# One concatenated FFN weight tensor, loads cut where a buffer is full, and two blocks of w_down loaded early in sixteen small DMAs

## The chip, the cores and the metric

The kernel runs on one core of a Trainium2 chip. The metric is device time in microseconds. The kernel before was timed in three runs: 815.88, 816.25 and 816.37 us, median 816.25 us. One further execution was taken with the hardware profiler; it is the source of all rows below.

## The reference

One token `x` of 1024 numbers goes through two branches. Branch a is attention with cached keys and values: 32 query heads, 4 key/value heads, 65,536 positions, head size 128, everything in float32.

```
q = (x @ wq) in 32 heads;  k, v = caches, each of 4 heads shared by 8 query heads
a = softmax(q k^T / sqrt(128)) v @ wo
```

Branch b is a feed-forward network (FFN) of width 3584 with a router weight and a residual:

```
r = x @ w_r
b = x + sigmoid(r) * ((silu(x @ w_gate) * (x @ w_up)) @ w_down)
g = sigmoid(sum(x * gate_w))
out = g * a + (1 - g) * b
```

With a single token the router's choice of the top token is always that token. The weights and the caches together are 346 MB, and each byte is used once.

## The kernel before

All large loads go through one pool, `stream`, with two buffers of 16,384 float32 a partition (64 KB a partition, 8 MB a buffer). `room` takes the next buffer, `load` takes one and fills it with one DMA. All of these DMAs are issued by SP (SyncE) in the order of the program. A DMA into a buffer waits until TensorE has read the buffer's previous contents; so two large loads are under way or in use at any time. The order of the program is the order of each engine's queue; no planner moves anything.

The four key/value heads are a loop over `g`. For each: `queries` (32 matmuls, L131), then four loads of keys with two chunks of 8192 positions each (`score_chunk`, L150), the maximum over all chunks (`neg_max`), four loads of values with two chunks each (`value_chunk`, L179), and `project`, which multiplies with this head's part of `wo` into the accumulator `att` (L202). The parts of wo for head g and of wq for head g + 1 come together in a full buffer, `wo_wq`. For the last head there is no next wq, and `wo3` alone is loaded: 4 MB into a buffer of 8 MB (`load(wo3, HG, D)`).

Behind the loop follows the FFN. `up_proj` runs twice, for w_gate and w_up. Each time it makes two loads of four rows of the weight (row: 3584 numbers a partition, 7 MB a load of four) and 64 matmuls a load (L239, sixteen a row). The result goes from PSUM to `row` through ScalarE (L244), and is turned by 14 small matmuls (L247). Then w_down comes in 28 blocks of 1024 numbers a partition (512 KB a block), in two buffers of 14 blocks: the first in one DMA, the second in six of 6, 4, 2, 1, 1/2 and 1/2 blocks (L270, list `cuts`). The two halves of the last block split it by output quarters. Each block takes four matmuls into `y` (L281), one for each quarter of the output, of 256 columns each.

`x_row`, four rows of 256 numbers, is loaded right behind the first w_down load (L272). VectorE makes `res` of it (L275, L276), adds `y` (`fin`, L286), and SP stores the output (L287).

The lines that matter below are SP's issues L71, L270 and L272, in this order; the matmuls L202, L239 and L281 that wait for the loads; and the instruction queue of TensorE, whose 3134 matmuls and 3134 weight loads are fetched from memory by the same DMA engines while the kernel runs.

Of the kernel before, what the change touches and what calls it, by code (L numbers as in the profile page):

```python
# [9 lines left out]
F32 = mybir.dt.float32  # L10
# [4 lines left out]
P = 128  # L15
D = 1024
G = 4
HG = 8
DH = 128
SK = 65536  # L20
F = 3584
# [6 lines left out]
KB = D // P  # L28
NQ = D // 4
FB = F // P  # L30
# [2 lines left out]


@with_exitstack
def gated_mix_kernel(ctx: ExitStack, tc: tile.TileContext, x, vecs, k_t, v, wq0, wo_wq, wo3, w_gate, w_up, w_down, out):

# [13 lines left out]
    nc = tc.nc  # L54
    const = ctx.enter_context(tc.tile_pool(name="const", bufs=1))
# [7 lines left out]
    def room(*shape):  # L63
        t = stream.tile([P, W], F32, name="st", tag="st")
        names = " ".join("abcd"[: len(shape)])
        t = t[:, : math.prod(shape)]
        return t.rearrange(f"p ({names}) -> p {names}", **dict(zip("abcd", shape))) if len(shape) > 1 else t

    def load(src, *shape):
        t = room(*shape)  # L70
        nc.sync.dma_start(t, src)  # L71
        return t
# [4 lines left out]
    x_row = const.tile([P, NQ], F32, name="x_row")  # L77
# [19 lines left out]
    xp = const.tile([P, KB, 32], F32, name="xp")  # L97
# [7 lines left out]
    hp = const.tile([P, FB, 32], F32, name="hp")  # L105
# [8 lines left out]
    ps = ps_1.tile([P, P], F32, name="ps_m", tag="m")  # L114
# [12 lines left out]
    def queries(g, wq_t):  # L127
        ps = ps_s.tile([P, 512], F32, name="ps_q", tag="s")
        for k in range(KB):
            for j in range(4):  # L130
                nc.tensor.matmul(  # L131
                    ps[32 * j : 32 * j + 32, :NQ], xp[:, k, :], wq_t[:, k, j * NQ : (j + 1) * NQ],
                    start=(k == 0), stop=(k == KB - 1),
                )
        q_sb = work.tile([P, NQ], F32, name="q_sb")
        nc.vector.tensor_copy(q_sb, ps[:, :NQ])  # L136
        pt = ps_1.tile([P, P], F32, name="ps_m", tag="m")
        for e in range(2):
            nc.tensor.matmul(pt[:, 4 * e : 4 * e + 4], q_sb[:, e * DH : (e + 1) * DH], sel4, start=True, stop=True)
        for s in range(4):  # L140
            nc.vector.tensor_copy(
                qp[:, g % 2, s, 8 * s : 8 * s + 8].rearrange("p (j e) -> p e j", e=2),
                pt[:, :HG].rearrange("p (e j) -> p e j", e=2),
            )

    def score_chunk(g, c, kt, mx):
        ps = ps_s.tile([P, 512], F32, name="ps_s", tag="s")
        for s in range(4):
            for j in range(4):
                nc.tensor.matmul(  # L150
                    ps[32 * j : 32 * j + 32, :], qp[:, g % 2, s, :], kt[:, s, j, :], start=(s == 0), stop=(s == 3)
                )
        t = scores.tile([P, 512], F32, name="s", tag="s")
        nc.scalar.activation(t, ps, AF.Copy)  # L154
        nc.vector.tensor_reduce(mx[:, c : c + 1], t, AX.X, ALU.max)  # L155
        return t

    def neg_max(mx):

        m1 = work.tile([P, 1], F32, name="m1")  # L160
        nc.vector.tensor_reduce(m1, mx, AX.X, ALU.max)
        md = work.tile([P, P], F32, name="md")
        nc.vector.tensor_scalar_mul(md, ident, m1)
        ps = ps_1.tile([P, P], F32, name="ps_m", tag="m")
        nc.tensor.matmul(ps, ones, md, start=True, stop=True)
        mh = work.tile([P, HG], F32, name="mh")
        nc.vector.tensor_reduce(mh, ps.rearrange("p (a h) -> p h a", h=HG), AX.X, ALU.max)
        nc.vector.tensor_mul(mh, mh, nsel)
        nb = work.tile([P, 1], F32, name="nb")
        nc.vector.tensor_reduce(nb, mh, AX.X, ALU.add)  # L170
        return nb

    def value_chunk(g, c, t, vt, nb, sums, acc):
        nc.scalar.activation(t, t, AF.Exp, bias=nb, scale=SCALE, accum_out=sums[:, c : c + 1])  # L174
        pt = work.tile([P, 512], F32, name="pt", bufs=3)
        nc.vector.transpose(pt, t)  # L176
        for m in range(NM):
            j = m % 4
            nc.tensor.matmul(  # L179
                acc[32 * j : 32 * j + 32, :], pt[:, 32 * m : 32 * m + 32], vt[:, 4 * m : 4 * m + 4, :],  # L180
                start=(c == 0 and m < 4), stop=(c == NCH - 1 and m >= NM - 4),
            )

    def project(g, acc, sums, wo_t):
# [15 lines left out]
        for h in range(HG):  # L200
            for j in range(4):
# [2 lines left out]
                    start=(g == 0 and h == 0), stop=(g == G - 1 and h == HG - 1),  # L204
                )

    for g in range(G):
        queries(g, wq_t)
        mx = work.tile([P, NCH], F32, name="mx")
        s_t = []  # L210
        for c in range(NCH):
            if c % 2 == 0:
                kt = load(k_t[g, c // 2], 2, 4, 4, 512)
            s_t.append(score_chunk(g, c, kt[:, c % 2], mx))
        nb = neg_max(mx)
        sums = work.tile([P, NCH], F32, name="sums")
        acc = ps_o.tile([P, 512], F32, name="acc", tag="o")
        for c in range(NCH):
            if c % 2 == 0:
                vt = load(v[g, c // 2], 2, NB, DH)  # L220
            value_chunk(g, c, s_t[c], vt[:, c % 2], nb, sums, acc)
        if g < G - 1:
            both = load(wo_wq[g], 2, 8, 1024)
            wo_t, wq_t = both[:, 0], both[:, 1]
        else:
            wo_t = load(wo3, HG, D)
        project(g, acc, sums, wo_t)

    def up_proj(w):

        ps = ps_1.tile([P, 2, 512], F32, name="ps_f", tag="f")
        n = F // 8
        for k0 in range(0, KB, 4):
            wt = load(w[:, k0 : k0 + 4, :], 4, F)
            for k in range(4):
                for e in range(2):
                    for j in range(4):
                        at = (2 * j + e) * n
                        nc.tensor.matmul(  # L239
                            ps[32 * j : 32 * j + 32, e, :n], xp[:, k0 + k, :], wt[:, k, at : at + n],  # L240
                            start=(k0 + k == 0), stop=(k0 + k == KB - 1),
                        )
        row = work.tile([P, 2 * n], F32, name="row")
        nc.scalar.activation(row.rearrange("p (e n) -> p e n", e=2), ps[:, :, :n], AF.Copy)  # L244
        pt = ps_s.tile([P, 512], F32, name="ps_t", tag="s")
        for m in range(FQ):
            nc.tensor.matmul(pt[:, 4 * m : 4 * m + 4], row[:, m * P : (m + 1) * P], sel4, start=True, stop=True)  # L247
        return pt[:, :FB]


    gps = up_proj(w_gate)
    hid = const.tile([P, FB], F32, name="hid")
    nc.scalar.activation(hid, gps, AF.Exp, scale=-1.0)
    nc.vector.tensor_scalar_add(hid, hid, 1.0)
    nc.vector.reciprocal(hid, hid)
    nc.vector.tensor_mul(hid, gps, hid)
    ups = up_proj(w_up)
    nc.vector.tensor_mul(
        hp[:, :, 0].rearrange("p (j m) -> p m j", j=4), ups.rearrange("p (m j) -> p m j", j=4),
        hid.rearrange("p (m j) -> p m j", j=4),  # L260
    )


    y = ps_o.tile([P, NQ], F32, name="y", tag="o")
    halves = [room(FB // 2, D) for _ in range(2)]
    cuts = [(0, 14, 0, 4), (14, 20, 0, 4), (20, 24, 0, 4), (24, 26, 0, 4), (26, 27, 0, 4), (27, 28, 0, 2), (27, 28, 2, 4)]
    for b0, b1, j0, j1 in cuts:
        i = b0 // (FB // 2)
        at = slice(b0 - i * (FB // 2), b1 - i * (FB // 2))
        nc.sync.dma_start(halves[i][:, at, j0 * NQ : j1 * NQ], w_down[:, b0:b1, j0 * NQ : j1 * NQ])  # L270
        if i == 0:
            nc.sync.dma_start(x_row.rearrange("(j r) n -> j r n", r=32)[:, 0, :], x.rearrange("(j n) -> j n", j=4))  # L272

    res = const.tile([P, NQ], F32, name="res")
    nc.vector.tensor_scalar_mul(res, x_row, rest[:, 0:1])  # L275
    nc.vector.scalar_tensor_tensor(res, att, gate, res, op0=ALU.mult, op1=ALU.add)  # L276
    for b0, b1, j0, j1 in cuts:
        i = b0 // (FB // 2)
        for b in range(b0, b1):
            for j in range(j0, j1):  # L280
                nc.tensor.matmul(  # L281
                    y[32 * j : 32 * j + 32, :], hp[:, b, :], halves[i][:, b - i * (FB // 2), j * NQ : (j + 1) * NQ],
                    start=(b == 0), stop=(b == FB - 1),
                )
    fin = const.tile([P, NQ], F32, name="fin")
    nc.vector.scalar_tensor_tensor(fin, y, rest[:, 1:2], res, op0=ALU.mult, op1=ALU.add)  # L286
    nc.sync.dma_start(out.rearrange("(j n) -> j n", j=4), fin.rearrange("(j r) n -> j r n", r=32)[:, 0, :])  # L287
# [30 lines left out]
```

## Time and profile before

| | |
|---|---|
| median of three runs | 816.25 us |
| profiled execution | 815.95 us, of which its span 814.2 us |
| TensorE matmul busy | 397.8 us, 49% of the span |
| mean granted TensorE clock | 0.73 |
| bytes moved by DMA | 346.47 MB, mean 426 GB/s |
| chain that ended last | DMA 72%, PE 25%, ACT 2%, DVE 1% |
| first data | some 1.7 us after the start of the span |
| last w_down data in use | 810.27 us (last group of matmuls) |
| output stored by | 814.2 us |

The span runs from the first instruction to the last; about 1.7 us of the execution lie around it. Sixteen DMA engines move all data. A load of 128 partitions puts eight rows on each of them, one after the other; a load is usable when the slowest of the sixteen has finished. "DMA share" in a row is the mean busy share of these engines in a stretch. Because a packet is counted in the stretch in which it starts, short stretches after a restart can show more than 1.

### The profile page before, as it was taken

The numbers are of one execution on the slowest core, as the hardware profiler recorded it, in microseconds if no ns is written. First come the engines' busy times: TensorE is split into PE (matmuls) and PEld (weight loads), VectorE is DVE, ScalarE is ACT, GpSimd is POOL, SyncE is SP. The second block draws the span as 40 slices with busy tenths as digits, with TensorE's granted clock in tenths as the row PEclk, the third lists the DMA queues.
The fourth block names the chain that finished last, engine by engine and source line by source line (L and its number), as shares of the span: only waits on it lengthen the run. The fifth ranks groups of instructions, "written<-read, shape, count | busy, mean of one in ns | idle before, by whom it ended". The sixth has DMA issues, their size and how long they took to land.

```text
span 814.2 us, 6731 instructions
## 1 busy us (share of the span) xinstructions
PE 397.8 (49%) x3134; PEld 129.6 (16%) x3134; DVE 64.4 (8%) x149; ACT 45.6 (6%) x101; POOL 0.7 (0%) x6
## 2 busy tenths in 40 slices
PE   3444444444444554454454554454444444645457
PEld 1111111112111111122111111131111111211123
DVE  1000120000000200000000200000001100000000
ACT  0000020000000300000000300000001200000000
POOL 0000000000000000000000000000000000000000
PEclk9677777676677667767777777767767766857669
DMA  9999999999999999999999999999999999899997
GB/s 413 413 460 410 419 455 422 439 425 426 442 431 442 419 432 435 438 432 426 441 432 425 435 431 432 442 415 445 426 435 439 419 445 419 355 424 448 415 428 293
DMA packets 7099, 346.47 MB, mean 426 GB/s; under 512 B 920, under 2 KB 928, under 8 KB 1312
## 3 DMA queue, kind: packets, MB, share of 16 engines
q1 hardware_dynamic: 6928, 346.04, 98.6%
q8 instruction: 24, 0.39, 0.2%
q10 hardware_dynamic: 144, 0.01, 0.0%
q14 instruction: 3, 0.02, 0.0%
HBM read 346.05 MB, written 0.00 MB: 425 GB/s over the span
## 4 chain that ended last, share of the span: by engine, by line
DMA 72%; PE 25%; ACT 2%; DVE 1%; issue 0%; SPq 0%; ACTq 0%
DMA st<-in_k_t 29%; DMA st<-in_v 22%; DMA st<-in_wo_wq 11%; PE acc L179 9%; PE ps_s L150 9%; DMA st<-in_w_gate 4%; DMA st<-in_w_up 3%; DMA st<-in_w_down 3%; PE att L202 3%; PE ps_f L239 2%; ACT s L174 1%; PE ps_q L131 1%; SPq L270 0%; DVE mx L155 0%; PE y L281 0%
## 5 line engine op out<-in xcount | busy, mean ns | idle before, releaser
L150 PE MATMUL ps_s<-st,qp 128*32 128x512 f32 x1024 | 145.9, 734 | 162.1 <-DMA st<-in_k_t 162.1
L179 PE MATMUL acc<-st,pt 128*32 128x512 f32 x1024 | 148.5, 745 | 123.2 <-DMA st<-in_v 123.2
L150 PEld LDWEIGHTS ps_s<-st,qp 128*32 128x32 f32 x1024 | 40.0, 131 | 264.7 <-issue 264.7
L179 PEld LDWEIGHTS acc<-st,pt 128*32 128x32 f32 x1024 | 38.4, 134 | 230.0 <-issue 185.1
L239 PE MATMUL ps_f<-st,xp 128*32 128x448 f32 x256 | 34.7, 712 | 36.8 <-DMA st<-in_w_gate 22.6
L154 ACT ACTIVATE s<-ps_s 128x512 f32<-128x512 f32 x32 | 19.1, 597 | 567.9 <-PE ps_s L150 567.9
L155 DVE TENSOR_REDUCE mx<-s 128x1 f32<-128x512 f32 x32 | 22.0, 686 | 290.0 <-ACT s L154 290.0
L176 DVE STREAM_TRANSPOSE pt<-s 128x512 f32<-128x512 f32 x32 | 22.7, 711 | 177.2 <-PE acc L179 173.4
L202 PE MATMUL att<-st,op 128*32 128x256 f32 x256 | 21.3, 505 | 25.1 <-DMA st<-in_wo_wq 24.6
L174 ACT ACTIVATE s<-s,nb 128x512 f32<-128x512 f32 x32 | 22.6, 707 | 10.4 <-DVE nb L170 10.4
L281 PE MATMUL y<-st,hp 128*32 128x256 f32 x224 | 16.0, 431 | 7.5 <-DMA st<-in_w_down 7.5
L239 PEld LDWEIGHTS ps_f<-st,xp 128*32 128x32 f32 x256 | 9.8, 140 | 60.7 <-issue 27.5
L131 PE MATMUL ps_q<-st,xp 128*32 128x256 f32 x256 | 17.1, 427 | 0.0
L202 PEld LDWEIGHTS att<-st,op 128*32 128x32 f32 x256 | 11.1, 144 | 33.7 <-issue 31.1
L192 PE MATMUL ps_m<-sel,lb 128*128 128x8 f32 x8 | 2.3, 357 | 28.9 <-DVE lb L188 28.9
L281 PEld LDWEIGHTS y<-st,hp 128*32 128x32 f32 x224 | 8.1, 123 | 15.1 <-DVE res L276 5.8
L131 PEld LDWEIGHTS ps_q<-st,xp 128*32 128x32 f32 x256 | 9.2, 122 | 6.8 <-issue 2.8
L244 ACT ACTIVATE row<-ps_f 128x896 f32<-128x896 f32 x2 | 1.8, 918 | 146.6 <-PE ps_f L239 146.6
L190 DVE COPY o_sb<-acc 128x512 f32<-128x512 f32 x4 | 2.8, 692 | 87.2 <-PE acc L179 87.2
L115 PE MATMUL ps_m<-dsum,ones 128*128 128x2 f32 x2 | 0.6, 364 | 13.8 <-DVE dsum L113 13.8
L192 PEld LDWEIGHTS ps_m<-sel,lb 128*128 128x128 f32 x8 | 2.0, 311 | 29.6 <-issue 29.6
L136 DVE COPY q_sb<-ps_q 128x256 f32<-128x256 f32 x4 | 1.7, 424 | 55.9 <-PE ps_q L131 55.9
(53 smaller groups left out, 47.2 us busy)
## 6 DMA issues: line engine op xcount, KB each, us to landing
st<-in_w_gate SPq DMA_DIRECT2D x2, 7168.0 KB, 25.5
st<-in_w_up SPq DMA_DIRECT2D x2, 7168.0 KB, 25.7
st<-in_w_down SPq DMA_DIRECT2D x1, 7168.0 KB
st<-in_wq SPq DMA_DIRECT2D x1, 4096.0 KB, 12.3
st<-in_wo SPq DMA_DIRECT2D x1, 4096.0 KB, 19.0
st<-in_w_down SPq DMA_DIRECT2D x1, 3072.0 KB, 15.6
st<-in_w_down SPq DMA_DIRECT2D x1, 2048.0 KB, 20.1
st<-in_w_down SPq DMA_DIRECT2D x1, 1024.0 KB, 22.2
```

The costliest lines, as they stand in the source:

```text
L131: nc.tensor.matmul(ps[32 * j : 32 * j + 32, :NQ], xp[:, k, :], wq_t[:, k, j * NQ : (j + 1) * NQ], start=(k == 0), stop=(k == KB - 1),)
L150: nc.tensor.matmul(ps[32 * j : 32 * j + 32, :], qp[:, g % 2, s, :], kt[:, s, j, :], start=(s == 0), stop=(s == 3))
L154: nc.scalar.activation(t, ps, AF.Copy)
L155: nc.vector.tensor_reduce(mx[:, c : c + 1], t, AX.X, ALU.max)
L174: nc.scalar.activation(t, t, AF.Exp, bias=nb, scale=SCALE, accum_out=sums[:, c : c + 1])
L176: nc.vector.transpose(pt, t)
L179: nc.tensor.matmul(acc[32 * j : 32 * j + 32, :], pt[:, 32 * m : 32 * m + 32], vt[:, 4 * m : 4 * m + 4, :], start=(c == 0 and m < 4), stop= ...
L190: nc.vector.tensor_copy(o_sb, acc.rearrange("p (s d) -> p s d", s=4))
L192: nc.tensor.matmul(ps[:, :HG], lb, sel8, start=True, stop=True)
L202: nc.tensor.matmul(att[32 * j : 32 * j + 32, :], op[:, h, :], wo_t[:, h, j * NQ : (j + 1) * NQ], start=(g == 0 and h == 0), stop=(g == G - ...
L239: nc.tensor.matmul(ps[32 * j : 32 * j + 32, e, :n], xp[:, k0 + k, :], wt[:, k, at : at + n], start=(k0 + k == 0), stop=(k0 + k == KB - 1),)
L281: nc.tensor.matmul(y[32 * j : 32 * j + 32, :], hp[:, b, :], halves[i][:, b - i * (FB // 2), j * NQ : (j + 1) * NQ], start=(b == 0), stop=( ...
```

## The change

The reference's FFN weights and the last head's wo are laid side by side, per partition, into one input tensor `tail`: wo3, then w_gate's eight rows, w_up's eight rows, and w_down's blocks 0 to 26, then the last block in two pieces, of columns 0 to 191 and 192 to 255 of each output quarter. A list `parts` holds their widths and `begins` where each begins. `load_rest(first, *ends)` takes one buffer and fills it, in one DMA per given end, with consecutive parts.

So buffers are filled without regard to which weight ends where:

| buffer | contents | numbers a partition |
|---|---|---|
| 1 | wo3, gate rows 0 and 1 | 15,360 |
| 2 | gate rows 2 to 5 | 14,336 |
| 3 | gate rows 6 and 7, up rows 0 and 1 | 14,336 |
| 4 | up rows 2 to 5 | 14,336 |
| 5 | up rows 6 and 7, w_down blocks 0 to 7 | 15,360 |
| 6 | w_down blocks 8 to 23, in DMAs of 8, 4, 2 and 2 blocks | 16,384 |
| 7 | w_down block 26, block 27 in two pieces (3/4 and 1/4) | 2,048 |

Blocks 24 and 25 of w_down are not in these loads. They have a tile of their own, `early` (8 KB a partition), which is filled by sixteen DMAs of eight partitions each, 8 KB a partition, 64 KB a DMA. The partitions of one such DMA are four apart (for instance 0, 4, ... 28). SP issues one of them behind every other load of keys and of values, four a head, over the whole attention loop.

The matmuls of w_down now begin with blocks 24 and 25. The last block's last matmuls have 64 columns instead of 256; there are four more matmuls in all. x_row is issued by SP behind buffer 6 instead of behind the first w_down load. The number of large buffers filled is seven as before, and the bytes are the same.

```
+    pieces = [(0, 192), (192, NQ)]
+    parts = [HG * D] + [F] * (2 * KB) + [D] * (FB - 1) + [4 * (c1 - c0) for c0, c1 in pieces]
+    begins = [sum(parts[:i]) for i in range(len(parts) + 1)]
+    rest_of = {}
+    def load_rest(first, *ends):
+        t = room(begins[ends[-1]] - begins[first])
+        a = first
+        for b in ends:
+            nc.sync.dma_start(
+                t[:, begins[a] - begins[first] : begins[b] - begins[first]], tail[:, begins[a] : begins[b]]
+            )
+            for i in range(a, b):
+                rest_of[i] = t[:, begins[i] - begins[first] : begins[i + 1] - begins[first]]
+            a = b
+    w0 = 1 + 2 * KB
+    b_early = 24
+    early = const.tile([P, 2, D], F32, name="early")
+    for i in range(2):
+        rest_of[w0 + b_early + i] = early[:, i, :]
+    eighths = [slice(32 * q + r, 32 * q + r + 29, 4) for r in range(4) for q in range(4)]
+    def load_eighth():
+        rows = eighths.pop()
+        a = begins[w0 + b_early]
+        nc.sync.dma_start(early[rows], tail[rows, a : a + 2 * D].rearrange("p (b n) -> p b n", b=2))
...
                 kt = load(k_t[g, c // 2], 2, 4, 4, 512)
+                if c % 4 == 2:
+                    load_eighth()
...
                 vt = load(v[g, c // 2], 2, NB, DH)
+                if c % 4 == 2:
+                    load_eighth()
...
-            wo_t = load(wo3, HG, D)
+            load_rest(0, 3)
+            wo_t = rest_of[0].rearrange("p (h n) -> p h n", h=HG)
...
-        for k0 in range(0, KB, 4):
-            wt = load(w[:, k0 : k0 + 4, :], 4, F)
+        for k in range(KB):
+            if first + k in loads:
+                load_rest(first + k, loads[first + k])
...
-    gps = up_proj(w_gate)
+    gps = up_proj(1, {3: 7, 7: 11})
...
-    ups = up_proj(w_up)
+    ups = up_proj(1 + KB, {11: 15, 15: 25})
...
+    load_rest(w0 + 8, w0 + 16, w0 + 20, w0 + 22, w0 + 24)
+    nc.sync.dma_start(x_row.rearrange("(j r) n -> j r n", r=32)[:, 0, :], x.rearrange("(j n) -> j n", j=4))
+    load_rest(w0 + 26, w0 + 27, w0 + 28, w0 + 29)
...
-    for b0, b1, j0, j1 in cuts:
-        i = b0 // (FB // 2)
-        for b in range(b0, b1):
-            for j in range(j0, j1):
-                nc.tensor.matmul(
-                    y[32 * j : 32 * j + 32, :], hp[:, b, :], halves[i][:, b - i * (FB // 2), j * NQ : (j + 1) * NQ],
-                    start=(b == 0), stop=(b == FB - 1),
-                )
+    order = [b_early, b_early + 1] + [b for b in range(FB - 1) if b not in (b_early, b_early + 1)]
+    for b in order:
+        for j in range(4):
+            nc.tensor.matmul(
+                y[32 * j : 32 * j + 32, :], hp[:, b, :], rest_of[w0 + b][:, j * NQ : (j + 1) * NQ],
+                start=(b == order[0]), stop=False,
+            )
+    for i, (c0, c1) in enumerate(pieces):
+        n = c1 - c0
+        for j in range(4):
+            nc.tensor.matmul(
+                y[32 * j : 32 * j + 32, c0:c1], hp[:, FB - 1, :], rest_of[w0 + FB - 1 + i][:, j * n : (j + 1) * n],
+                start=False, stop=(c1 == NQ),
+            )
```

More of the change, by code (lines that the diff above doesn't have):

```diff
@@ L35, in gated_mix_kernel @@
 @with_exitstack
-def gated_mix_kernel(ctx: ExitStack, tc: tile.TileContext, x, vecs, k_t, v, wq0, wo_wq, wo3, w_gate, w_up, w_down, out):
+def gated_mix_kernel(ctx: ExitStack, tc: tile.TileContext, x, vecs, k_t, v, wq0, wo_wq, tail, out):
     nc = tc.nc
@@ L225, in gated_mix_kernel, with up_proj @@
         else:
-            wo_t = load(wo3, HG, D)
+            load_rest(0, 3)
+            wo_t = rest_of[0].rearrange("p (h n) -> p h n", h=HG)
         project(g, acc, sums, wo_t)
-    def up_proj(w):
+    def up_proj(first, loads):
         ps = ps_1.tile([P, 2, 512], F32, name="ps_f", tag="f")
         n = F // 8
-        for k0 in range(0, KB, 4):
-            wt = load(w[:, k0 : k0 + 4, :], 4, F)
[L235 to L241, printed above, removed]
-                        )
+        for k in range(KB):
+            if first + k in loads:
+                load_rest(first + k, loads[first + k])
+            for e in range(2):
+                for j in range(4):
+                    at = (2 * j + e) * n
+                    nc.tensor.matmul(
+                        ps[32 * j : 32 * j + 32, e, :n], xp[:, k, :], rest_of[first + k][:, at : at + n],
+                        start=(k == 0), stop=(k == KB - 1),
+                    )
         row = work.tile([P, 2 * n], F32, name="row")
@@ L261, in gated_mix_kernel @@
     )
+    load_rest(w0 + 8, w0 + 16, w0 + 20, w0 + 22, w0 + 24)
+    nc.sync.dma_start(x_row.rearrange("(j r) n -> j r n", r=32)[:, 0, :], x.rearrange("(j n) -> j n", j=4))
+    load_rest(w0 + 26, w0 + 27, w0 + 28, w0 + 29)
     y = ps_o.tile([P, NQ], F32, name="y", tag="o")
-    halves = [room(FB // 2, D) for _ in range(2)]
-    cuts = [(0, 14, 0, 4), (14, 20, 0, 4), (20, 24, 0, 4), (24, 26, 0, 4), (26, 27, 0, 4), (27, 28, 0, 2), (27, 28, 2, 4)]
-    for b0, b1, j0, j1 in cuts:
-        i = b0 // (FB // 2)
[L269 to L272, printed above, removed]
     res = const.tile([P, NQ], F32, name="res")
@@ L276, in gated_mix_kernel @@
     nc.vector.scalar_tensor_tensor(res, att, gate, res, op0=ALU.mult, op1=ALU.add)
-    for b0, b1, j0, j1 in cuts:
-        i = b0 // (FB // 2)
-        for b in range(b0, b1):
-            for j in range(j0, j1):
-                nc.tensor.matmul(
-                    y[32 * j : 32 * j + 32, :], hp[:, b, :], halves[i][:, b - i * (FB // 2), j * NQ : (j + 1) * NQ],
-                    start=(b == 0), stop=(b == FB - 1),
-                )
+    order = [b_early, b_early + 1] + [b for b in range(FB - 1) if b not in (b_early, b_early + 1)]
[7 more added lines that the diff above has]
+        n = c1 - c0
+        for j in range(4):
+            nc.tensor.matmul(
+                y[32 * j : 32 * j + 32, c0:c1], hp[:, FB - 1, :], rest_of[w0 + FB - 1 + i][:, j * n : (j + 1) * n],
+                start=False, stop=(c1 == NQ),
+            )
     fin = const.tile([P, NQ], F32, name="fin")
@@ L297 @@
     wo = a["A_wo"].reshape(G, HG, P, D).transpose(0, 2, 1, 3)
+    down = a["B_w_down"].reshape(FB, P, D).transpose(1, 0, 2)
+    last = down[:, -1].reshape(P, 4, NQ)
     arrays = {
@@ L304 @@
         "wo_wq": np.stack([wo[:-1], wq[1:]], axis=2),
-        "wo3": wo[-1],
-        "w_gate": a["B_w_gate"].reshape(P, KB, F),
-        "w_up": a["B_w_up"].reshape(P, KB, F),
-        "w_down": a["B_w_down"].reshape(FB, P, D).transpose(1, 0, 2),
+        "tail": np.concatenate(
+            [wo[-1].reshape(P, -1), a["B_w_gate"].reshape(P, -1), a["B_w_up"].reshape(P, -1)]
+            + [down[:, :-1].reshape(P, -1), last[:, :, :192].reshape(P, -1), last[:, :, 192:].reshape(P, -1)],
+            axis=1,
+        ),
     }
```

## The prediction

> **What bounds the kernel now.** I read the page first: busy shares, queues, shares of the chain.
>
> ```profile
> span 814.2 us, 6731 instructions
> PE 397.8 (49%) x3134; PEld 129.6 (16%) x3134; DVE 64.4 (8%) x149; ACT 45.6 (6%) x101; POOL 0.7 (0%) x6
> ...
> q1 hardware_dynamic: 6928, 346.04, 98.6%
> q8 instruction: 24, 0.39, 0.2%
> ```
>
> TensorE is busy half of the time; the sixteen DMA engines are busy practically always with q1, the loads that SP issues. The change keeps the bytes, so it can win only where these engines stand still or end unequally. For that I cut the end of the span into stretches (columns: stretch, length, busy time of PE, PEld, DVE, ACT and POOL, granted clock, DMA share, GB/s; a packet counts in the stretch in which it starts).
>
> ```profile
> 600.00:690.00 90.00, 45.33 (x320) 12.38 (x312) 9.94 (x19) 8.14 (x20) 0.00 (x0) 0.73 1.00 431
> 699.00:700.20 1.20, 1.20 (x20) 0.34 (x12) 0.00 (x0) 0.00 (x0) 0.00 (x0) 1.00 0.63 259
> 700.20:701.40 1.20, 1.20 (x16) 0.34 (x12) 0.00 (x0) 0.00 (x0) 0.00 (x0) 1.00 0.53 218
> 701.40:702.60 1.20, 1.20 (x16) 0.40 (x12) 0.00 (x0) 0.00 (x0) 0.00 (x0) 1.00 0.51 218
> 702.60:703.80 1.20, 1.20 (x16) 0.27 (x8) 0.00 (x0) 0.00 (x0) 0.00 (x0) 1.00 0.26 109
> 703.80:705.20 1.40, 0.59 (x6) 0.21 (x2) 0.69 (x1) 0.00 (x0) 0.00 (x0) 1.00 0.00 0
> 803.30:806.90 3.60, 2.64 (x52) 1.21 (x40) 0.00 (x0) 0.00 (x0) 0.00 (x0) 1.00 0.99 401
> 807.80:808.25 0.45, 0.45 (x12) 0.28 (x12) 0.00 (x0) 0.00 (x0) 0.00 (x0) 1.00 0.54 205
> 808.25:809.80 1.55, 1.31 (x22) 0.31 (x14) 0.00 (x0) 0.00 (x0) 0.00 (x0) 1.00 0.25 95
> 809.80:812.00 2.20, 1.07 (x8) 0.14 (x4) 0.48 (x1) 0.00 (x0) 0.00 (x0) 1.00 0.00 0
> ```
>
> Up to 690 the share is 1.00. Then there is a staircase. A row of 1.20 us is about one packet of the 32 KB that a partition of wo3 has, since 431 GB/s over 16 engines is 26.9 KB a us. From 700.2 to 702.6 the share is about 0.5: eight engines still work, eight are done since about 700.3 to 701. From 702.6 it is 0.26: four. Those stop by about 704.4, and nothing starts until 705.2. At the very end it is 0.25 again: four engines work until 809.8, the other twelve are done at about 808.0. Somebody takes time from eight engines, and unequally. The instruction queue is the one candidate on the page (the share of 16 engines is the last column):
>
> ```profile
> q8 instruction: 20, 0.33, 0.2%
> ```
>
> for 0 to 704 us,
>
> ```profile
> q8 instruction: 4, 0.07, 0.3%
> ```
>
> for 705 to 804 us, and for 763 to 765 us, around one of them,
>
> ```profile
> q8 instruction: 1, 0.02, 3.3%
> ```
>
> A fetch of 16 KB holds one engine for 0.033 x 16 x 2 = 1.06 us. Twenty fetches dealt in turn to eight engines make three on four engines and two on four: the staircase 8, 4, 4. Its steps (about 700.3, 703.2, 704.4) give some 1.4 us a fetch. Four fetches after the gap fit the four late engines at the end. That it is always the same eight is my reading, not a row.
>
> The gap itself is explained by the chain of waits and SP's issues.
>
> ```profile
> 695.49 8.73 PE acc L179 x64
> ...
> 706.56 3.71 PE att L202 x64
> ...
> 810.27 0.65 PE y L281 x4
> ```
>
> ```profile
> 686.01 0.33 SPq L71 DMA_DIRECT2D st<-in_wo  x1
> 704.24 6.37 SPq L71 DMA_DIRECT2D st<-in_w_gate  x2
> ...
> 767.87 0.68 SPq L272 DMA_DIRECT2D x_row<-in_x  x1
> ```
>
> The load of wo3 is only 4 MB, 9.7 us at 431 GB/s. It is over before TensorE has released the other buffer (695.49 + 8.73 = 704.2), so the first w_gate load is issued at 704.24 into an empty queue. Its data were usable late too:
>
> ```profile
> 723.81 9.03 PE L239 MATMUL ps_f<-st,xp 128*32 128x448 f32 x64 [13.59 <-DMA st<-in_w_gate]
> ```
>
> 7168 KB are 17.0 us. From 705.2 that is 722.2; the end shows some 0.47 us from the last packet (809.8) to its matmuls (810.27). So 723.8 is 1.1 us late, up to 0.4 of it stagger: the restart costs each engine about 0.7 us.
>
> **The change, part by part.**
>
> *Fuller buffers.* wo3 becomes a DMA of 7.5 MB with two rows of w_gate behind it (61,440 B a partition, 18.2 us on each engine). Before 704.2 nothing differs in when it is issued. Now even the engines that end first have 8.4 us of work left at 700.3, until 708.7, and the next load is there by 705.2. The gap and the restart go. What is late next: wo is not usable until the whole DMA lands, at 705.3 + 8.4 + 0.5 = 714.2 where an engine also has the early rows (below). att needs it, and started at 706.56. From there: att 3.7, two rows of gate 4.5 (half of the 9.03 of a load), buffer free at 722.4, next load running at 723.4, while the other buffer lasts until 730.7: cover 7. The tightest later point is the buffer with two rows of gate and two of up.
>
> ```profile
> L244 ACT ACTIVATE row<-ps_f 128x896 f32<-128x896 f32 x2 | 1.8, 918 | 146.6 <-PE ps_f L239 146.6
> L247 PE MATMUL ps_t<-sel,row 128*128 128x4 f32 x28 | 3.4, 254 | 2.1 <-ACT row L244 2.1
> ```
>
> It lands near 748; 4.5 + 0.9 + 1.7 + 4.5 of work end at 759.6, and one microsecond later the load runs; the other buffer ends at 764.7. Cover about 4 us; without it the queue would stand still for what is missing. The last load, 1 MB, needs the buffer of up's last rows and eight blocks: landing 783.3, up 4.5, row and transposes 2.9, ten blocks 2.8 (160 of the y matmuls ran in 11.15 us in the row below), free at 793.5; the 8 MB in the other buffer last until about 802. Cover 8 us.
>
> ```profile
> 793.06 11.15 PE L281 MATMUL y<-st,hp 128*32 128x256 f32 x160 [5.75 <-DMA st<-in_w_down]
> 791.53 0.35 DVE L275 TENSOR_SCALAR res<-x_row,rest 128x256 f32<-128x256 f32 x1 [3.98 <-DMA x_row<-in_x]
> ```
>
> *x_row* is issued behind the 8 MB instead of behind the first w_down load, and lands near 802.5 instead of 791.5. Two operations of VectorE, under 0.9 us, follow; fin needs them near 806. Cost nothing, cover some 2.5 us. SP's issues behind it wait for a buffer anyway.
>
> *Sixteen early DMAs.* Each moves eight partitions x 8 KB. SP issues each right behind a large load, some 0.4 us of SP, before its next wait for a buffer, and such waits are long:
>
> ```profile
> SPq L71 <- PE acc L179: 150.9, 16, 10.8
> SPq L71 <- PE ps_s L150: 148.2, 16, 10.0
> ```
>
> So the issue is hidden by up to 10 us. Their semaphores come from the same eight in turn; what they make later DMAs wait for is long done. On the engines: they take 2 of 28 blocks off the last loads, 64 KB or 2.4 us from each of 16 engines, and put 16 rows of 8 KB on those that carry them. At the rate of the stretch with small packets (401 GB/s, 25 KB a us) a row is 0.33 us. The bounds are 0.30 (8 KB at 431 GB/s) and, as a hold with nothing in parallel, the 2.6 us that the lone first load had beyond its 9.7 us of bytes:
>
> ```profile
> st<-in_wq SPq DMA_DIRECT2D x1, 4096.0 KB, 12.3
> ```
>
> I take 0.33, since from 803.3 to 806.9 DMA follows DMA at a share of 0.99. Which engines? x_row, with four rows, made four packets of its own, on engines that went straight on (790.3 to 791.0 us, four packets between 512 B and 2 KB):
>
> ```profile
> DMA packets 31, 0.33 MB, mean 474 GB/s; under 512 B 15, under 2 KB 19, under 8 KB 19
> ```
>
> Eight rows then go to eight engines, and if these are the same each time, eight engines get 5.3 us and eight none. Whether those are the eight without fetches no row tells. I take it, with its chance below: an engine that had had a fetch since the gap would have been some 1.4 us behind with its 1 KB packet, and all four lie within 0.7 us. That is weak. [...]
>
> *Last pieces.* The last matmuls take 64 columns instead of 256: 0.65 us becomes between 0.16 and 0.65; I take 0.35, a gain of 0.3. Four matmuls more lie under the loads.
>
> **The sum, by engine, for the end of the data** (809.8 now). Four with a fetch after the gap: 809.8 - 2.0 (idle from about 703.2) - 0.7 (restart) - 2.4 = 804.7. Four with three fetches before it: 808.0 - 0.8 - 0.7 - 2.4 = 804.1. Eight without: 808.0 - 4.9 (from 700.3) - 0.7 - 2.4 + 5.3 = 805.3. The last counts: 805.3, a gain of 4.5, and 0.3 of the last piece: 4.8. The profiled execution took 815.95 us, so 811.15; the median of the runs shown, 816.25, lies 0.3 above it: 811.4.
>
> **The rivals.**
> 1. *The rows go to the engines with the fetches, or to a mixed half.* Then 804.7 + 5.3 = 810.0: 0.2 later than now, less 0.3: 816.1, no change. For it: no row names a half. Against: the x_row engines, weakly.
> 2. *The rows spread over all sixteen.* 804.7 + 2.65 = 807.4, a gain of 2.4 + 0.3: 813.5. Against: it would need another choice of engines each time.
> 3. *Slower: each small DMA holds its engines beyond its bytes.* At 0.33 us the gain is 4.8; each 0.1 more costs 1.6. It is lost at 0.63, and the kernel is measurably slower from 0.73 us on; at 1.0 us it is 811.4 + 16 x 0.67 = 822.1. For it: the 2.6 us of the lone load. Against: the 0.99 while 1 MB, 0.5 MB and 0.25 MB loads follow each other. [...]
> 4. *The gap moves to a later load,* where the tight cover of 4 us fails: 811.4 plus what is missing; 2 us give 813.4.
>
> **How the numbers follow.** Forecast 0.62 (own range 810.4 to 812.6: restart 0.4 to 1.1, row 0.30 to 0.38, last piece); spread or a small later gap 0.11; wrong half 0.18; slower by held engines 0.09. Under about 0.2%, 1.6 us, a measurement cannot tell a change here. Faster takes the first two and a little of the third, 0.74; same 0.17; slower 0.09. The range, 810.4 to 816.4, leaves out the slower case and tails.
>
> **What would show it.** Right: DMA share near 1.00 from 699 to 716; the first att matmul near 714 instead of 706.56; no engine done before 804; the staircase at the end under 1 us. Wrong half: a share of 0.5 or less for the last 8 us or so, with the data ending near 810. Held engines: landings of the large loads some 0.3 us or more later per early DMA already in the first 600 us. A moved gap: a stretch of low share near 760.

## The result and the profile after

The changed kernel takes 820.07 us (median of six runs, 818.98 to 820.49) against 816.38 us before (six runs, 815.88 to 817.65): a ratio of 1.0039, 95% interval 1.0026 to 1.0052. It is slower by 3.7 us. Forecast were 811.4 us with a range of 810.4 to 816.4; the time lies outside it, and on the other side.

The profiled execution took 818.98 us. From its page:

```profile
span 817.2 us, 6762 instructions
DMA packets 7355, 346.47 MB, mean 424 GB/s; under 512 B 1048, under 2 KB 1184, under 8 KB 1440
q8 instruction: 24, 0.39, 0.2%
```

Same bytes, same 24 fetches, a lower mean rate (424 against 426 GB/s). The stretches of the changed kernel, with the columns of the prediction:

```profile
699.00:716.00 17.00, 9.98 (x72) 3.42 (x72) 1.07 (x3) 0.00 (x0) 0.00 (x0) 0.76 1.00 428
810.00:811.00 1.00, 1.00 (x24) 0.60 (x20) 0.00 (x0) 0.00 (x0) 0.00 (x0) 1.00 0.55 208
811.00:812.00 1.00, 1.00 (x28) 0.52 (x21) 0.00 (x0) 0.00 (x0) 0.00 (x0) 1.00 0.24 92
812.00:813.00 1.00, 1.00 (x24) 0.44 (x16) 0.00 (x0) 0.00 (x0) 0.00 (x0) 1.00 0.12 44
```

For the same first stretch the kernel before has

```profile
699.00:716.00 17.00, 9.90 (x124) 4.29 (x112) 1.07 (x3) 0.00 (x0) 0.00 (x0) 0.90 0.80 327
```

So the gap is gone: 1.00 in place of 0.80, 3.4 us of every engine's time. But the staircase at the end is there, later than before: at 810 to 811 us about nine of sixteen engines work, then four, then two. The chain of waits shows the delay earlier (start, duration, what):

```profile
684.08 8.41 PE acc L178 x64
692.51 29.31 DMA st<-in_tail
721.95 6.48 PE att L201 x64
...
766.25 25.06 DMA st<-in_tail
791.31 0.04 issue
791.35 5.54 PE ps_f L276 x32
...
799.98 13.23 PE y L312 x216
813.21 0.01 issue
813.22 0.71 PE y L319 x16
```

att begins at 721.95, where the prediction had 714; the buffer with up's last rows and eight blocks of w_down lands at 791.3 instead of 783.3. So 8 us were lost before the end began, most of them before 692 us, while the attention loop ran: the load with wo starts at 692.51 instead of 686.01, and the load of keys that lands at 617.55 in the kernel before lands at 623.64, 6.1 us later with thirteen early DMAs ahead of it. From 791 on the matmuls of the last steps follow each other without a wait, and meet the last data at 813.

Where the 8 us went can be seen beside single early DMAs. Two stretches of 6 us, each with one early DMA in it, the first behind a load of keys (226 to 232 us), the second behind a load of values (305 to 311 us), rows of the load queue (packets, MB, share of 16 engines):

```profile
q1 hardware_dynamic: 68, 2.49, 104.2%
...
q1 hardware_dynamic: 68, 2.56, 98.7%
```

Divide engine time by bytes: 1.042 x 16 x 6 / 2.49 = 40.2 us of engine time for a MB in the first, 0.987 x 96 / 2.56 = 37.0 in the second. 37.0 is what packets of 64 KB in 2.42 us come to (16 engines at 433 GB/s). The extra 3.2 times 2.49 MB is 8 us of engine time, half a microsecond on each of the sixteen engines. The records of single packets in the trace say it directly: behind a load of keys the packets of 64 KB that run beside the early rows take 0.1 to 0.65 us longer than their 2.42 us, on all sixteen engines, the eight that carry no early rows too; behind a load of values none does. The early rows themselves take 0.31 to 0.50 us. Over the eight early DMAs behind keys, the extra time of these packets adds up to 62 us of engine time, 3.9 us for each engine. The two kinds differ in one more thing: `eighths` is emptied from its end, so each head's two DMAs behind keys write partitions from 64 up, and its two behind values write partitions under 64.

The records name no engine, but most packets start 3 or 4 ns before another ends, and joined so they make sixteen chains, each with eight packets of every load of 128 rows: the engines. In the fifteen early DMAs before 692 us it is each time the same eight that carry a row. Two of these eight are among the eight that fetch instructions (fetches at 117, 378 and 667 us; 156 and 416), six are not. The starts of the early rows show it too: from one early DMA to the next, one of the eight falls back against the others by some 1.6 us over the fetch at 117, and again over that at 416, and none by more than 0.1 us over those at 78 and 627.

### The profile page after: what moved, and what is told of

Same layout as the page of the kernel before. It is cut to its first block, busy times and chain, and to the rows that moved or that the text cites. A ratio compares the mean times of both kernels' runs of the same rounds, so it can differ in the third digit from the quotient of the medians.

```text
span 817.2 us, 6762 instructions
## 1 busy us (share of the span) xinstructions
PE 396.5 (49%) x3142; PEld 129.6 (16%) x3142; DVE 64.4 (8%) x149; ACT 45.6 (6%) x101; POOL 0.7 (0%) x6
## 4 chain that ended last, share of the span: by engine, by line
DMA 72%; PE 25%; ACT 1%; issue 0%; DVE 0%; SPq 0%; ACTq 0%
DMA st<-in_k_t 30%; DMA st<-in_v 26%; DMA st<-in_tail 10%; PE ps_s L149 9%; PE acc L178 9%; DMA st<-in_wo_wq 7%; PE att L201 2%; PE ps_f L276 2%; PE y L312 2%; PE ps_q L130 1%; ACT s L173 1%; PE ps_t L284 0%; ACT row L281 0%; PE y L319 0%; DVE mx L154 0%
## 5 line engine op out<-in xcount | busy, mean ns | idle before, releaser
L178 PE MATMUL acc<-st,pt 128*32 128x512 f32 x1024 | 146.7, 737 | 126.1 <-DMA st<-in_v 126.1
L201 PE MATMUL att<-st,op 128*32 128x256 f32 x256 | 25.2, 579 | 33.3 <-DMA st<-in_wo_wq 25.6
L201 PEld LDWEIGHTS att<-st,op 128*32 128x32 f32 x256 | 13.1, 165 | 43.9 <-issue 43.3
L312 PE MATMUL y<-st,hp 128*32 128x256 f32 x200 | 11.5, 392 | 0.0
L312 PEld LDWEIGHTS y<-st,hp 128*32 128x32 f32 x200 | 6.3, 115 | 5.4 <-issue 1.1
```

Source lines behind the costliest of these rows:

```text
L178: nc.tensor.matmul(acc[32 * j : 32 * j + 32, :], pt[:, 32 * m : 32 * m + 32], vt[:, 4 * m : 4 * m + 4, :], start=(c == 0 and m < 4), stop= ...
L201: nc.tensor.matmul(att[32 * j : 32 * j + 32, :], op[:, h, :], wo_t[:, h, j * NQ : (j + 1) * NQ], start=(g == 0 and h == 0), stop=(g == G - ...
L312: nc.tensor.matmul(y[32 * j : 32 * j + 32, :], hp[:, b, :], rest_of[w0 + b][:, j * NQ : (j + 1) * NQ], start=(b == order[0]), stop=False,)
```

## The experiments

Theory A: the partitions that an early DMA writes decide whether it slows all engines (with eight rows, those from 64 up do), and the engines that carry both fetches and early rows, two in the changed kernel, set the end. Rival B: the place behind key loads costs the time. Rival C: the rows read in memory cost it. Rival D: the fuller buffers lose, not the early DMAs. Times of runs on different chips are compared as differences to the kernel before on the same chip.

**The fuller buffers alone** (e1): `early` and `load_eighth` go, and the blocks of w_down are used in their order.

```
-                if c % 4 == 2:
-                    load_eighth()
...
-    load_rest(w0 + 26, w0 + 27, w0 + 28, w0 + 29)
+    load_rest(w0 + 24, w0 + 26, w0 + 27, w0 + 28, w0 + 29)
```

> The fuller buffers alone: blocks 24 and 25 come with the last buffer, no early DMAs. Theory A (the gap at 704 us is won as predicted, the early DMAs lose more than that): by the prediction's sum without the shift the four engines with a late fetch end at 809.8 - 2.0 - 0.7 = 807.1 and the last piece saves 0.3, so about 813.4 us, 3 us under before. Rival (the fuller buffers win nothing, or lose, because a later load starts late): 816 us or more, with a stretch of low DMA share between 706 and 800 us.

Measured: 813.18 us against 816.36, ratio 0.9966 (0.9953 to 0.9978). By the time rival D falls; its sign, a stretch of low share, is there all the same and is shown below. The same kernel once more, on another chip (e9):

> The kernel of e1_no_early once more, beside the other: about 813.2 us again. It is complete, and the fastest so far of those that are.

Measured: 813.73 us against 817.28, ratio 0.9962 (0.9948 to 0.9975). The gap and the end of this kernel, in stretches:

```profile
699.00:716.00 17.00, 9.79 (x84) 3.99 (x80) 1.07 (x3) 0.00 (x0) 0.00 (x0) 0.70 1.00 429
806.00:807.00 1.00, 0.79 (x16) 0.16 (x8) 0.00 (x0) 0.00 (x0) 0.00 (x0) 1.00 0.35 130
807.00:808.00 1.00, 0.64 (x20) 0.32 (x16) 0.00 (x0) 0.00 (x0) 0.00 (x0) 1.00 0.03 11
```

The data end at about 807, for which the prediction's sum without the shift gives 809.8 - 2.0 - 0.7 = 807.1. But one later load did start late. The load with up's last rows is issued at 760.81 (the prediction had its buffer free at 759.6), and ahead of it the share is low:

```profile
759.00:761.00 2.00, 1.74 (x20) 0.28 (x12) 0.00 (x0) 0.00 (x0) 0.00 (x0) 0.93 0.58 238
```

By the packet records eight of the sixteen engines run out of work at 758.8 to 759.9 and stand still for 2 to 4 us; the others go on with hardly a pause. In the profiled execution of e9 the pauses there are 0.6 us at most, and some engines pause for 0.7 to 1.9 us near 798 instead. The end is set by engines that were late anyway, so the data still end where the sum has them. This version is complete and faster than both kernels.

**The early DMAs alone** (e7): the kernel before, with `early`, `load_eighth` and its two calls, blocks 24 and 25 taken out of `cuts`.

```
+                if c % 4 == 2:
+                    load_eighth()
...
-cuts = [..., (20, 24, 0, 4), (24, 26, 0, 4), (26, 27, 0, 4), ...]
+cuts = [..., (20, 24, 0, 4), (26, 27, 0, 4), ...]
```

> The kernel before with the sixteen early DMAs alone (read from w_down, same rows and places as in the changed kernel), the loads otherwise cut as before. Theory A (the two parts add up): 816.4 + (820.1 - 813.2) = about 823.3 us. Rival (the early rows fill the gap at 704 us on the engines that are done early, so that they cost less there): under 820 us.

Measured: 822.67 us against 816.83, ratio 1.0061 (1.0040 to 1.0082). Early rows cost 5.8 us alone and 3.7 + 3.2 = 6.9 beside fuller buffers. The parts add up within the intervals.

**The order turned** (e2)

```
-    eighths = [slice(32 * q + r, 32 * q + r + 29, 4) for r in range(4) for q in range(4)]
+    eighths = [slice(32 * q + r, 32 * q + r + 29, 4) for r in range(4) for q in (2, 3, 0, 1)]
```

> The order of the early DMAs within a head is turned: behind key loads now go partitions under 64, behind value loads those from 64 up. In the changed kernel every early DMA behind a key load (rows from partition 64 up) made the 64 KB packets of all sixteen engines about 0.3 to 0.6 us longer, those behind value loads did not. Theory A (the partitions written decide): the time stays near 820 us and the long packets move to the value loads. Rival B (the key loads decide): 820 us too, but the long packets stay at the key loads.

Measured: 820.82 us against 816.36, ratio 1.0054 (1.0038 to 1.0070). The same two stretches:

```profile
q1 hardware_dynamic: 70, 2.56, 98.7%
...
q1 hardware_dynamic: 67, 2.56, 106.5%
```

Now 226 to 232 us, behind the keys, is undisturbed (37.0 us of engine time a MB) and 305 to 311, behind the values, is slow (39.9). The delay follows the partitions. Rival B falls.

**All partitions under 64, all from 64 up** (e3, e4)

```
+    nc.vector.memset(early, 0.0)
+    other = const.tile([P, 2, D], F32, name="other")
+    early2 = [early, other]
+    eighths = [(q // 2, slice(32 * (q % 2) + r, 32 * (q % 2) + r + 29, 4)) for r in range(4) for q in range(4)]
...
-        rows = eighths.pop()
+        i, rows = eighths.pop()
+        dst = slice(rows.start + 0, rows.stop + 0, 4)      # e3; in e4 + 64 in place of + 0
+        src = slice(rows.start + 0, rows.stop + 0, 4)
...
-        nc.sync.dma_start(early[rows], tail[rows, a : a + 2 * D].rearrange("p (b n) -> p b n", b=2))
+        nc.sync.dma_start(early2[i][dst], tail[src, a : a + 2 * D].rearrange("p (b n) -> p b n", b=2))
```

> All sixteen early DMAs read and write partitions 0 to 63, half of them into a second tile that is not used; partitions 64 to 127 of blocks 24 and 25 stay zero, so this part of w_down is left out of the sum. Same bytes, same engines. Theory A (eight DMAs to partitions from 64 up cost all engines some 0.5 us each): 820.1 - 4.2 = about 816 us. Rival B (the place behind key loads costs it): 820 us.

> All sixteen early DMAs write partitions 64 to 127 but read the rows of partitions 0 to 63 from memory, so blocks 24 and 25 hold zeros in the lower half and other rows' weights in the upper half. Theory A, cause in the partitions written: 820.1 + 4.2 = about 824 us. Theory C, cause in the rows read from memory: about 816 us, as with the lower rows in e3_lower. Rival B (key loads): 820 us.

Measured: e3 815.06 us against 816.36, ratio 0.9985 (0.9976 to 0.9995); e4 823.45 us, ratio 1.0087 (1.0072 to 1.0103). The two stretches of e3, then of e4:

```profile
q1 hardware_dynamic: 69, 2.75, 106.2%
...
q1 hardware_dynamic: 48, 2.39, 92.2%
```

```profile
q1 hardware_dynamic: 67, 2.36, 98.0%
...
q1 hardware_dynamic: 66, 2.29, 98.8%
```

Engine time a MB is 37.1 and 37.0 in e3, 39.9 and 41.4 in e4. Both read the same rows, so rival C falls: the partition written decides. Sixteen DMAs of eight rows to partitions from 64 up against none cost 823.45 - 815.06 = 8.4 us, 0.52 us each. The changed kernel has eight of them: 4.2 us by this, 5.0 by its own distance from e3 (3.69 + 1.30 against the kernel before).

**Four rows a DMA** (e5, e8; e8 with the second tile of e3)

In e5 the DMAs behind keys write partitions 16 to 31 and 48 to 63, those behind values 0 to 15 and 32 to 47; in e8 all write 0 to 15 and 32 to 47, half of them in a second tile that nothing reads, and the rest of blocks 24 and 25 stays zero.

```
-    eighths = [slice(32 * q + r, 32 * q + r + 29, 4) for r in range(4) for q in range(4)]
+    eighths = [slice(32 * q + u + r, 32 * q + u + r + 13, 4) for r in range(4) for u in (0, 16) for q in (0, 1)]   # e5
+    eighths = [(i, slice(32 * q + r, 32 * q + r + 13, 4)) for r in range(4) for i in (0, 1) for q in (0, 1)]       # e8
```

> The sixteen early DMAs have four partitions x 8 KB instead of eight, all under partition 64; the upper halves of blocks 24 and 25 stay zero, so that part of w_down is left out. Each engine that carries them has the same 16 rows as in e3_lower, but these are four engines instead of eight. Theory A (three of the eight engines of e3_lower also carry instruction fetches, and set its end; the four that four-row DMAs use carry none): by the prediction's sum the data end near 805.3, and the time is about 811.4 to 812.5 us, under e3_lower's 815.1. Rival (the early rows cost what they cost on any engine): 815 us as e3_lower. [...]

> [...] Theory A (a foreign partition slows all engines, and the first four engines carry no fetches): the 0.35 us that each of the eight DMAs behind key loads cost in e5_four_rows goes, so 814.3 - 2.8 = about 811.5 us, which is what the prediction forecast for the change. Rival (the place behind key loads costs it after all, whatever the partitions): 814.3 us.

"Foreign" in theory A of e8 rests on an assumption of the author's about which engine writes which partition. No run shows that, nor which engines are the first four and that they carry no fetches. Theory A of e5 counts three engines with fetches and early rows; in the changed kernel they are two.

Measured: e5 814.29 us against 816.83, ratio 0.9973 (0.9964 to 0.9983); e8 812.38 us against 817.28, ratio 0.9937 (0.9925 to 0.9950). e5 lay above the 811.4 to 812.5 that its theory A gives for fetches alone, and its rows say why. e8 was forecast at 811.5 us, as a gain of 2.8 us over e5; measured against each one's own kernel before, the gain is 2.4. The two stretches of e5, then of e8:

```profile
q1 hardware_dynamic: 58, 2.39, 96.6%
...
q1 hardware_dynamic: 62, 2.79, 107.4%
```

```profile
q1 hardware_dynamic: 58, 2.65, 102.3%
...
q1 hardware_dynamic: 46, 2.57, 99.1%
```

In e5, behind the keys, it is 38.8 us a MB, though partitions 16 to 31 and 48 to 63 lie in the lower half. In e3 the same partitions were written by DMAs of eight rows, and nothing slowed down (37.1 and 37.0). So it is not the partition alone that decides, but the partition together with the number of rows; why, no run shows. In e8, with partitions 0 to 15 and 32 to 47 alone, 37.1 and 37.0. Against the kernel before e5 gains 2.5 us and e8 4.9: eight DMAs of four rows to partitions 16 to 31 and 48 to 63 cost 2.4 us, 0.3 each. And e8 against e3, both undisturbed in both stretches, gains 4.9 - 1.3 = 3.6 us more. By theory A that is what the engines with fetches and early rows cost; that the engines of e8's early rows have no fetches is its assumption. The load with up's last rows shows the same distance: it lands at 787.24 in e3 and at 783.59 in e8, and in e3 nothing from there to the end waits for data. The ends of e3 and of e8, in stretches:

```profile
806.00:807.00 1.00, 1.00 (x24) 0.58 (x20) 0.00 (x0) 0.00 (x0) 0.00 (x0) 1.00 0.70 264
807.00:808.00 1.00, 1.00 (x24) 0.65 (x20) 0.00 (x0) 0.00 (x0) 0.00 (x0) 1.00 0.21 82
808.00:809.00 1.00, 1.00 (x28) 0.57 (x21) 0.00 (x0) 0.00 (x0) 0.00 (x0) 1.00 0.12 44
```

```profile
804.00:806.00 2.00, 1.26 (x20) 0.58 (x24) 0.29 (x1) 0.00 (x0) 0.00 (x0) 1.00 0.57 214
806.00:807.00 1.00, 0.67 (x16) 0.16 (x8) 0.00 (x0) 0.00 (x0) 0.00 (x0) 1.00 0.07 26
```

In e3 some three engines work on after 807 (0.21 of sixteen), two until nearly 809 (0.12), as many as carry both in the changed kernel; in e8 all but one are done by 806 (0.07). e8 is not a kernel to keep, since it leaves out part of w_down and carries half a MB less in all.

**Four rows, complete** (e6): e5 plus one DMA of 64 partitions for the missing halves.

```
+    nc.sync.dma_start(early[64:P], tail[64:P, a : a + 2 * D].rearrange("p (b n) -> p b n", b=2))
     load_rest(w0 + 8, w0 + 16, w0 + 20, w0 + 22, w0 + 24)
```

> As e5_four_rows, but complete: the upper halves of blocks 24 and 25 are loaded by one DMA of 64 partitions just ahead of the last large buffer. Theory A: the four engines without fetches take 5.3 us of the others' work; by engine the data end near 806.5 instead of 807.1 in e1_no_early, so about 812.6 us, hardly to be told from e1_no_early's 813.2. Rival (as in e5_four_rows): 815 us or more.

Measured: 818.85 us against 816.83, ratio 1.0024 (1.0015 to 1.0033). The forecast missed by 6 us. Two terms are in it: eight early DMAs as in e5 (2.4 to 2.8 us), and the DMA of 64 rows, all to partitions from 64 up. Around that DMA, 778 to 800 us:

```profile
q1 hardware_dynamic: 357, 8.66, 99.0%
```

0.99 x 16 x 22 / 8.66 = 40.2 us of engine time a MB instead of 37.0, that is 1.7 us on each engine. The profiled execution, 817.58 us, was the shortest of the ten. In it the data end at 811.1, by its packet records, where theory A had 806.5, and the two terms are 4.1 to 4.5 of these 4.6 us. The median lies 1.3 us above this execution; why e6 varies that much stays open.

## Why the prediction was wrong, step by step

- *What bounds the kernel: right.* The DMA engines bound it; eight of them lose time to instruction fetches (0.94 to 1.11 us each), in turn, and (by the joined records) always the same eight; and the gap was the buffer that wo3 left half empty.
- *Fuller buffers: right, in mechanism and size.* Without the early DMAs the prediction's terms give 813.4, a gain of 2.9 us; measured were gains of 3.18 (e1) and 3.55 (e9). Rival 4 came true in part and cost nothing: in e1 eight engines stand still for 2 to 4 us near 760, the place that it names. The cover of 4 us was worked out for engines with early rows, which end the load of wo at 713.7. Engines that have neither early rows nor fetches end it at 708.7 by the prediction, and three loads of 17.0 us later, at 759.7, they run dry before the next load runs at 760.6. They are not the ones that set the end.
- *The step that failed is the cost of the sixteen early DMAs.* It priced the rows rightly (0.33 us each; measured in the changed kernel 0.31 behind loads of values, 0.33 on average) but charged only the eight engines that carry them. The time that an early DMA takes from all the other engines it put at nothing, without a reason. Eight of the sixteen DMAs cost every engine about half a microsecond each, 4 to 5 us in all. Rival 3 had asked whether an early DMA costs more than its bytes, but only on the engines that carry it. Its sign, landings later by 0.3 us or more for each early DMA within the first 600 us, did appear (6.1 us for thirteen at 617 us), without its mechanism. What was held against it, the small last loads, have 128 rows each and could not show what a DMA of eight rows does to the other engines.
- *Which engines carry the rows: the 0.18 of rival 1 was the true case, in its mixed form.* The rows go to the same eight engines each time, as the sum takes it, but two of the eight have fetches too; two are the last to finish, and this cost some 3.6 us (e8 against e3). Its price, 816.1, was 4.7 over the forecast. The evidence of the x_row packets was called weak and was: it was of four engines, and even for these no row shows that they have no fetches.
- *The sum.* Add both to the forecast: 811.4 + 3.6 + 5.0 = 820.0; measured 820.1. Both terms are differences between runs, and together they are the distance of the changed kernel from e8. So this agreement says only that e8, which has neither cost, gained 4.9 us, where the forecast for the change was 4.8. The traces give the split on their own: 3.9 us an engine of longer packets, and the load with up's last rows landing at 783.6 in e8, 787.2 in e3 and 791.3 in the changed kernel, where the prediction had 783.3.
- *Issue and semaphores: right.* SP's early issues cost nothing that shows: e8, 4.9 us under the kernel before, has the same sixteen issues.
- *A term mis-sized without effect on the verdict:* ten blocks of y were put at 2.8 us. Each matmul appears as two instructions in the rows, so ten blocks are x80, and took 4.57 us (e8) to 6.24 us (e6). The cover of 8 us for the last load was nearer 5 in e8. In the changed kernel it was gone: the load is issued at 805.95, and the share from 806 to 808 is 0.89. Its last matmuls run without a pause from 799.98 to 813.9 all the same, so that earlier data at the very end would not have helped by much.
- *The range.* It put 0.09 on slower. The two mishaps were held to be alternatives; they came together, and the dearer of them had no rival of its own.

## What to carry to other kernels

Where all sixteen DMA engines are the bound, as here, the engine with the most work sets the end (two of them until 813 us in the changed kernel), so look at how many are still busy in the last microseconds and in each gap, not only at the mean share. A DMA over part of the partitions need not be free beside large loads even where its bytes are few (0.5 us on every engine for 64 KB in e4, nothing beyond its bytes in e3): compare the packets beside it for other partitions and other numbers of rows, or leave its rows in a load of 128. And before work is moved onto engines that seem idle, find out which engines it will land on; here filling the buffers alone (0.9966) beat filling them and balancing (1.0039).

## What the runs showed of the hardware that was not expected

- A DMA with eight rows of 8 KB to partitions from 64 up makes the packets of all sixteen engines longer (up to 3.07 us instead of 2.42 in the changed kernel) and costs about 0.5 us an engine (e4 against e3); one with four rows to partitions 16 to 31 or 48 to 63 costs 0.3 us (e5 against e8). Eight rows to partitions under 64 (e3), or four to 0 to 15 and 32 to 47 (e8), leave the engine time at 37.0 to 37.1 us a MB, and in the changed kernel a row under 64 takes 0.31 to 0.32 us. No run shows the cause.
- An instruction fetch of 16 KB takes an engine 0.94 to 1.11 us (changed kernel, mean 1.05), and the 64 KB packet behind it takes 2.89 to 2.97 us instead of 2.42 (nineteen fetches up to 667 us). The 24 fetches go in turn to eight engines; by the joined records two of these are among the eight that an eight-row DMA uses.
- Unequal engines added up over the kernel before as long as no buffer ran empty: at the gap the engines with no fetch end at 699.8 to 700.9 us, those with two at 702.9 to 703.3 and those with three at 704.2 to 704.6 (joined records), 1.5 us a fetch with the longer packet behind it. Where the queue does run empty, near 760 us in e1 (share 0.58 from 759 to 761), the engines that are ahead stand still and the late ones do not, so that the end does not move.
